# Moving the last output's matmuls and copies behind a data-dependent branch, with the last three stores

## The chip, the cores and the metric

One NeuronCore of a Trainium2 chip runs the kernel; the other cores are idle. The metric is the device time of one execution in microseconds. Five engines run their own instruction streams: TensorE (PE in the profile, with its weight loads as a row of their own, PEld), VectorE (DVE), ScalarE (ACT), GpSimd (POOL) and SyncE (SP), which issues the DMA transfers. They wait for each other through semaphores.

## The reference

A gated linear attention feeds a gated MLP with a spatial product. What is computed:

```python
f = 1.0 / (1.0 + np.exp(-f_logit))
for t in range(S):
    state = f[:, :, t, :, None] * state + np.einsum('bhd,bhe->bhde', k[:, :, t], v[:, :, t])
    y[:, :, t] = np.einsum('bhd,bhde->bhe', q[:, :, t], state)
...
h = np.maximum(x @ w_in, 0.0)
u, v = (h[..., :d_ff // 2], h[..., d_ff // 2:])
v_n = (v - mu) / np.sqrt(var + 1e-06)
v_s = np.einsum('ts,bsd->btd', w_spatial, v_n) + b_spatial[None, :, None]
gated = u * v_s
return (gated @ w_out).astype(np.float32)
```

There are 4 batches, 8 heads of 48 channels, 768 tokens, a model width of 384 and a hidden width of 1024, all in float32.

## The kernel before

The attention runs chunk by chunk with closed-form products in place of the step-by-step recurrence. The MLP works on halves of 384 tokens (`th`) and, for the output, on tiles of 128 tokens (`tt`, three in each half). Every product of the MLP is made in three passes over operands that were split into a high and a low part (`gh`, `gl` for the gated values, `w_outh`, `w_outl` for the weights), and all passes of one output add up in one PSUM bank out of four, `mm0` to `mm3`.

The order of all work is written out by hand in the list `PLAN`: words such as `S:3,1,3` name a step and its indices, and the program runs them one after the other. Each engine executes its own instructions in this order. The steps at the end of the list are:

- `sg`, `sm`, `sh`, `sl` (L607 to L622): for one of four slices of the gated values, bias, product, high part (ACT, `gh`) and low part (DVE, `gl`).
- `Oa:b,th,tt` and `O:b,th,tt` (`part_O`, L631 to L646): the output product of one tile, `gated @ w_out`. `Oa` makes the passes over the first three slices, 9 products; `O` adds the fourth slice, 3 products, or makes all 12 if no `Oa` came before. The very last output, named by `LAST`, is made in two halves of 192 columns in two banks, so it has twice as many products of half the width.
- `oc` (L648 to L653): ACT copies a finished bank to one of three buffers `osb`; the last output is copied half by half.
- `od` (L655 to L658): SP issues the store of an `osb` buffer, 192 KB.
- `end` is no step. It marks the place in `PLAN` where the branch stands.

The closed form of the attention is not exact for extreme forget gates. A check counts such entries, every engine loads the count into a register (`load`, in the middle of the program), and after the steps ahead of `end` there is a branch on it (L716): the first arm repeats everything in a general, slow way; the second arm, the usual one, runs the steps behind `end`. The branch is an instruction of each of the five streams. The first arm lies between the branch and the second arm in every stream. Before the change the second arm holds three stores:

```python
    with tc.If(n_bad > 0) as found:
        ...
    osbs = outputs
    with found.Else():
        for what in PLAN[stop + 1:]:
            run(what)
```

Of the kernel before, what the change touches and what calls it, by code (L numbers as in the profile page):

```python
# [29 lines left out]
P = 128  # L30
# [73 lines left out]
    sg:3,0,0 oc:2,1,0 od:2,1,0 sm:3,0,0 S:3,0,1 sl:3,0,2 sg:3,0,1 S:3,1,3 od:2,0,0 sh:3,0,0 sl:3,0,0 sm:3,0,1  # L104
    U:3,1,0 S:3,1,0 sg:3,1,0 sh:3,0,1 sl:3,0,1 O:3,0,1 oc:3,0,1 od:3,0,1 ur:3,1,0 sm:3,1,0 sh:3,1,0 sl:3,1,0 U:3,1,1
    O:3,0,0 oc:3,0,0 U:3,1,2 ur:3,1,2 ur:3,1,1 sm:3,1,1 O:3,0,2 sh:3,1,1 sl:3,1,1 sm:3,1,2 sh:3,1,2 sl:3,1,2
    oc:3,0,2 U:3,1,3 sg:3,1,3 ur:3,1,3 sm:3,1,3 Oa:3,1,1 Oa:3,1,2 sh:3,1,3 sl:3,1,3 O:3,1,2 oc:3,1,2 Oa:3,1,0
    od:3,0,0 od:3,0,2 O:3,1,0 oc:3,1,0 O:3,1,1 oc:3,1,1 end od:3,1,2 od:3,1,0 od:3,1,1
""".split()


# [36 lines left out]
def tile_kernel(ctx, tc, fkq, fn, vv, w_cv, w_spT, b_sp, out):  # L148
# [6 lines left out]
    ps = ctx.enter_context(tc.tile_pool(name="ps", bufs=1, space=PSUM))  # L155

    def tiles(pool, name, count, shape, dtype=F32):
        return [pool.tile(shape, dtype, name=f"{name}{i}") for i in range(count)]
# [24 lines left out]
    sB = tiles(attn, "sB", 2, [DP, J * D])  # L183
    ysb = attn.tile([P, HD], F32, name="ysb")

    mm = Slots(tiles(ps, "mm", 4, [P, 512]))
    bp = Slots(tiles(ps, "bp", 2, [P, 2, 512]))
    xTs = Slots([tuple(const.tile([P, KX, TH], F32R, name=f"xT{k}{i}") for k in "hl") for i in range(3)])
    vrs = Slots(tiles(const, "vr", 3, [P, G]))
# [5 lines left out]
    gs = gts = osbs = None  # L195
# [459 lines left out]
    def step_od(b, th, tt, row=None):  # L655
        at = (b if row is None else row) * S + th * TH + tt * P
        nc.sync.dma_start(out[bass.ds(at, P)], osbs.of((b, th, tt)))
        osbs.done((b, th, tt))  # L658
# [52 lines left out]


    attn_pool.close()
    outputs = osbs
    dram = ctx.enter_context(tc.tile_pool(name="dram", bufs=1, space=bass.MemoryType.DRAM))
    with tc.If(n_bad > 0) as found:  # L716
        xd = dram.tile([B, HD, S], F32, name="xd")
# [46 lines left out]
        with tc.tile_pool(name="again", bufs=1) as again:  # L764
            open_moe(again)
            xf = again.tile([P, KX, TH], F32, name="xf")
            with tc.For_i(0, B) as b:
# [19 lines left out]
                for th in range(2):  # L787
# [3 lines left out]
                    for tt in range(HU):  # L791
                        step_O("b", th, tt)
                        step_oc("b", th, tt)
                        step_od("b", th, tt, b)
    osbs = outputs
    with found.Else():
        for what in PLAN[stop + 1:]:
            run(what)
# [45 lines left out]
```

## Time and profile before

| what | us |
|---|---|
| median of 3 runs | 352.29 |
| lowest and highest run | 351.34, 353.19 |
| the profiled execution, its own time | 352.25 |
| span of the profiled execution | 350.4 |
| PE busy | 334.1 |
| last copy of the last output ends | 345.1 |
| last store issued | 345.2 |

The span runs from the first to the last instruction in the trace; the execution's own time is 1.85 us longer. Times within the span count from its start. A weight load and its matmul are two instructions, shown under PEld and PE. The instruction streams themselves arrive by DMA, on queues that the profile calls "instruction": q8 with packets of 16 KB, q14 with packets of 8 KB. Rows with a q behind the engine (PEldq, ACTq, SPq) belong to an engine's sequencer, the part that reads the stream and hands work to the engine.

### The profile page before, as it was taken

What the parts mean: (1) busy time and instruction counts of PE and PEld (TensorE: products, weight loads), DVE (VectorE), ACT (ScalarE), POOL (GpSimd) and SP (SyncE); (2) the same over time, 40 slices, a digit from 0 to 9 for tenths busy, and PEclk for the clock granted to TensorE, in tenths of its full rate; (3) what the DMA queues carried; (4) which work ended last, traced back from release to release, by engine and by line L of the source; (5) the groups of instructions that cost most, each with busy time, mean ns of one, the idle gap of its engine ahead of it and who ended that gap; (6) DMA issues with size and microseconds to landing.
All of it is one profiled execution on the core that took longest, in us unless ns stands there. A gap on an engine that the chain in (4) does not pass through costs nothing.

```text
span 350.4 us, 10471 instructions
## 1 busy us (share of the span) xinstructions
PE 334.1 (95%) x4590; PEld 311.7 (89%) x4590; DVE 218.7 (62%) x436; ACT 171.4 (49%) x349; POOL 46.4 (13%) x69
## 2 busy tenths in 40 slices
PE   4689999999999999999999999999999999999993
PEld 3577888989999899999889989999989989999993
DVE  2799879999896966446574675535557657132140
ACT  7776799683645645124544754233443534121231
POOL 3123111303200101003020030012001200001100
PEclk9899999999999999999999999999999999999998
DMA  7849485745323503021630332400101000001012
GB/s 246 331 116 296 153 291 167 281 145 160 91 93 116 204 1 137 2 74 64 178 118 2 125 106 87 159 2 1 47 4 45 4 22 24 22 7 40 23 49 74
DMA packets 14981, 36.01 MB, mean 103 GB/s; under 512 B 1488, under 2 KB 10192, under 8 KB 14928
## 3 DMA queue, kind: packets, MB, share of 16 engines
q1 hardware_dynamic: 14928, 35.26, 30.3%
q8 instruction: 38, 0.62, 0.8%
q14 instruction: 15, 0.12, 0.1%
HBM read 30.54 MB, written 4.72 MB: 101 GB/s over the span
## 4 chain that ended last, share of the span: by engine, by line
PE 89%; DMA 4%; ACT 2%; DVE 1%; issue 1%; SPq 1%; POOL 0%; ACTq 0%; DVEq 0%
PE mm L598 29%; PE mm L636 15%; PE mm L499 14%; PE mm L584 13%; PE bp L385 5%; PE bp L437 4%; PE bp L449 3%; PE bp L409 2%; PE mm L462 2%; DMA fkq<-fkq 2%; DMA words<-w_cv 2%; PE mm L340 2%; POOL fkq L325 0%; DVE fkq L357 0%; SPq L311 0%
## 5 line engine op out<-in xcount | busy, mean ns | idle before, releaser
L607 DVE TENSOR_TENSOR gt<-mm,b_bc 128x384 f32<-128x384 f32 x32 | 17.7, 553 | 37.7 <-PE mm L598 37.7
L598 PE MATMUL mm<-w_sph,vnh 128*128 128x384 f32 x192 | 40.1, 344 | 0.5 <-ACT vr L513 0.5
L598 PE MATMUL mm<-w_spl,vnh 128*128 128x384 f32 x192 | 39.0, 338 | 0.0
L598 PE MATMUL mm<-w_sph,vnl 128*128 128x384 f32 x192 | 39.0, 338 | 0.0
L598 PEld LDWEIGHTS mm<-w_sph,vnh 128*128 128x128 f32 x192 | 33.4, 188 | 0.9 <-ACT vr L513 0.6
L598 PEld LDWEIGHTS mm<-w_spl,vnh 128*128 128x128 f32 x192 | 34.2, 188 | 0.0
L598 PEld LDWEIGHTS mm<-w_sph,vnl 128*128 128x128 f32 x192 | 34.2, 188 | 0.0
L614 POOL TENSOR_TENSOR uT<-gt,uT 128x384 f32<-128x384 f32 x12 | 14.1, 1176 | 149.0 <-DVE gt L607 97.7
L589 ACT ACTIVATE uT<-mm 128x384 f32<-128x384 f32 x32 | 15.5, 489 | 27.4 <-PE mm L584 27.4
L618 ACT CAST gh<-uT 128x384 fp32r<-128x384 f32 x32 | 16.0, 511 | 21.1 <-DVE uT L614 13.4
L622 DVE TENSOR_TENSOR gl<-uT,gh 128x384 fp32r<-128x384 f32 x32 | 17.4, 555 | 13.0 <-ACT gh L618 13.0
L385 PE MATMUL bp<-q,fkq 48*64 48x112 f32 x768 | 23.4, 260 | 0.4 <-DVE fkq L357 0.4
L325 POOL TENSOR_SCALAR fkq<-fkq 112x512 f32<-112x512 f32 (+1 forms) x11 | 16.7, 1515 | 53.4 <-DMA fkq<-fkq 21.7
L584 PE MATMUL mm<-xTh,w_inh 128*128 128x384 f32 x96 | 23.0, 347 | 0.0
L652 ACT COPY osb<-mm 128x384 f32<-128x384 f32 (+1 forms) x25 | 11.4, 465 | 23.6 <-PE mm L636 23.6
L361 DVE TENSOR_TENSOR q<-fkq,F 112x512 f32<-112x512 f32 x24 | 16.4, 684 | 9.6 <-ACT F L346 7.9
L636 PE MATMUL mm<-w_outh,gh 128*128 128x384 f32 (+1 forms) x100 | 22.3, 337 | 0.0
L636 PE MATMUL mm<-w_outh,gl 128*128 128x384 f32 (+1 forms) x100 | 22.1, 333 | 0.0
L584 PE MATMUL mm<-xTh,w_inl 128*128 128x384 f32 x96 | 22.1, 338 | 0.0
L584 PE MATMUL mm<-xTl,w_inh 128*128 128x384 f32 x96 | 22.0, 338 | 0.0
L499 PE MATMUL mm<-w_inh,xTh 128*128 128x512 f32 x72 | 21.8, 410 | 0.0
L636 PE MATMUL mm<-w_outl,gh 128*128 128x384 f32 (+1 forms) x100 | 21.6, 331 | 0.0
(106 smaller groups left out, 704.0 us busy)
## 6 DMA issues: line engine op xcount, KB each, us to landing
fkq<-fkq SPq DMA_DIRECT2D x16, 768.0 KB, 4.6
val<-vv SPq DMA_DIRECT2D x24, 192.0 KB, 4.4
out<-osb SPq DMA_DIRECT2D x24, 192.0 KB, 2.0
fkq<-fkq SPq DMA_DIRECT2D x8, 512.0 KB, 6.0
words<-w_cv SPq DMA_DIRECT2D x4, 768.0 KB, 6.6
fkq<-fn SPq DMA_DIRECT2D x8, 192.0 KB, 3.2
late<-w_cv SPq DMA_DIRECT2D x2, 768.0 KB, 5.7
spat<-w_spT SPq DMA_DIRECT2D x3, 384.0 KB, 5.0
```

Source lines behind the costliest of these rows:

```text
L325: (nc.gpsimd if beside("c", n) else nc.vector).tensor_scalar(f, f, -LOGIT_MOST, None, op0=ALU.max)
L361: nc.vector.tensor_tensor(qs[n % 2][:, :, :, 0:C], *(x.rearrange("p (j c t) -> p j c t", c=T // C, t=C) for x in (parts(n)[2], Fs[n % 2])) ...
L385: nc.tensor.matmul(sc[to, e, cs], k[dr, at:at + C], qs[n % 2][dr, j, chunk], start=True, stop=True)
L499: nc.tensor.matmul(acc, xs[:, c, ut * P:(ut + 1) * P], ws[:, c, G:FF], start=i == 0, stop=i == 3 * KX - 1)
L584: nc.tensor.matmul(acc[:, 0:TH], ws[:, kx, cs], xs[:, kx, :], start=i == 0, stop=i == 3 * KX - 1)
L589: nc.scalar.activation(uTs.take((b, th, c)), mm.of(("u", b, th, c))[:, 0:TH], AF.Relu)
L598: nc.tensor.matmul(acc[:, 0:TH], vns.of((b, ks))[va][:, cs], w_sp_s[wb][:, ks, th * TH:(th + 1) * TH], start=i == 0, stop=i == 3 * KS - 1,)
L607: nc.vector.tensor_tensor(gts.take((b, th, c)), mm.of(("s", b, th, c))[:, 0:TH], b_bc[:, th * TH:(th + 1) * TH], op=ALU.add)
L614: (nc.vector if beside("sm", b, th, c) else nc.gpsimd).tensor_tensor(uT, gts.of((b, th, c)), uT, op=ALU.mult)
L618: nc.scalar.copy(gs.take((b, th, c), HU)[0], uTs.of((b, th, c)))
L622: nc.vector.tensor_tensor(lo, uTs.of((b, th, c)), hi.bitcast(F32), op=ALU.subtract)
L636: nc.tensor.matmul(acc[:, ms], gs.of((b, th, c))[ga][:, ts], w_out_s[wb][:, c, ms], start=c == cs[0] == 0 and ga == wb == 0, stop=c == cs[ ...
```

## The change

The list `PLAN` ends differently, and the four banks and the pools that the second arm uses are kept aside while the first arm is recorded.

```diff
-    oc:3,0,2 U:3,1,3 sg:3,1,3 ur:3,1,3 sm:3,1,3 Oa:3,1,1 Oa:3,1,2 sh:3,1,3 sl:3,1,3 O:3,1,2 oc:3,1,2 Oa:3,1,0
-    od:3,0,0 od:3,0,2 O:3,1,0 oc:3,1,0 O:3,1,1 oc:3,1,1 end od:3,1,2 od:3,1,0 od:3,1,1
+    oc:3,0,2 U:3,1,3 sg:3,1,3 ur:3,1,3 sm:3,1,3 Oa:3,1,2 Oa:3,1,0 sh:3,1,3 sl:3,1,3 O:3,1,2 oc:3,1,2 od:3,0,0
+    od:3,0,2 O:3,1,0 oc:3,1,0 end O:3,1,1 oc:3,1,1 od:3,1,2 od:3,1,0 od:3,1,1
...
-    mm = Slots(tiles(ps, "mm", 4, [P, 512]))
+    banks = tiles(ps, "mm", 4, [P, 512])
+    mm = Slots(banks)
...
-    outputs = osbs
+    mine = mm, gs, gts, osbs
+    mm = Slots(banks)
...
-    osbs = outputs
+    mm, gs, gts, osbs = mine
```

On PE before, ahead of the branch, the last products stand in this order (`mm2` is tile 3,1,0; `mm1` and `mm3` are the halves of the last output, tile 3,1,1, whose other 18 products stand at the head of the final 48):

```order
L636 MATMUL mm2_132<-w_outh_75,gh3_1340 128x384
L636 MATMUL mm2_132<-w_outl_76,gh3_1340 128x384
L636 MATMUL mm2_132<-w_outh_75,gl3_1341 128x384
L636 MATMUL mm1_131<-w_outh_75,gh3_1340 128x192
L636 MATMUL mm1_131<-w_outl_76,gh3_1340 128x192
L636 MATMUL mm1_131<-w_outh_75,gl3_1341 128x192
L636 MATMUL mm3_133<-w_outh_75,gh3_1340 128x192
L636 MATMUL mm3_133<-w_outl_76,gh3_1340 128x192
L636 MATMUL mm3_133<-w_outh_75,gl3_1341 128x192
L716 COMPARE_AND_BRANCH
L724 COMPARE_AND_BRANCH
```

On PE after the change, at the same place (`mm1` is now tile 3,1,2 and `mm3` tile 3,1,0, each begun by 9 products ahead of these rows):

```order
L637 MATMUL mm1_131<-w_outh_75,gh3_1340 128x384
L637 MATMUL mm1_131<-w_outl_76,gh3_1340 128x384
L637 MATMUL mm1_131<-w_outh_75,gl3_1341 128x384
L637 MATMUL mm3_133<-w_outh_75,gh3_1340 128x384
L637 MATMUL mm3_133<-w_outl_76,gh3_1340 128x384
L637 MATMUL mm3_133<-w_outh_75,gl3_1341 128x384
L718 COMPARE_AND_BRANCH
L726 COMPARE_AND_BRANCH
```

And on PE after the change, at the end of the second arm, which was empty of products before (`mm0` and `mm2` are the halves of the last output; 24 products in all, of which the last five stand here):

```order
L637 MATMUL mm2_132<-w_outl_76,gh3_1340 128x192
L637 MATMUL mm2_132<-w_outh_75,gl0_1335 128x192
L637 MATMUL mm2_132<-w_outh_75,gl2_1339 128x192
L637 MATMUL mm2_132<-w_outh_75,gl1_1337 128x192
L637 MATMUL mm2_132<-w_outh_75,gl3_1341 128x192
L718 UNCONDITIONAL_BRANCH
```

Between the product of slice 2 of the gated values and the branch PE had 48 products, 24 of 384 columns and 24 of 192. Now the 24 wide ones stand ahead of the branch and the 24 narrow ones behind it.

On ACT before, around the branch, from the last high part on:

```order
L618 CAST gh3_1340<-uT3_165 128x384
L652 COPY osb2_1349<-mm0_130 128x384
L652 COPY osb1_1348<-mm2_132 128x384
L652 COPY osb0_1347<-mm1_131 128x192
L652 COPY osb0_1347<-mm3_133 128x192
L716 COMPARE_AND_BRANCH
```

And on ACT after the change, at the same place:

```order
L619 CAST gh3_1340<-uT3_165 128x384
L653 COPY osb2_1349<-mm1_131 128x384
L653 COPY osb1_1348<-mm3_133 128x384
L718 COMPARE_AND_BRANCH
L726 COMPARE_AND_BRANCH
```

The two narrow copies now stand in the second arm. SP's stream is the same in both kernels: the three last stores stand in the second arm, in the order 3,1,2, then 3,1,0, then 3,1,1. DVE and POOL have no work moved.

## Rows read from the trace of the kernel before

**Rows 1.** The page's head and part 1: busy us, share of span, instructions.

```profile
span 350.4 us, 10471 instructions
...
PE 334.1 (95%) x4590; PEld 311.7 (89%) x4590; DVE 218.7 (62%) x436; ACT 171.4 (49%) x349; POOL 46.4 (13%) x69
```

**Rows 2.** The chain that ended last, from 340 us: start us, us, what.

```profile
339.92 4.20 PE mm L636 x24
...
344.56 0.55 ACT osb L652 x2
```

**Rows 3.** SP's timeline, stretch 345.2 to 346: start us, us, instruction.

```profile
345.20 0.33 SPq L657 DMA_DIRECT2D out<-osb  x1
```

**Rows 4.** SP's waits: us in total, times, longest us.

```profile
SPq L840 <- DMA out<-osb: 3.2, 2, 2.5
```

**Rows 5.** Stores issued at 338.2, 342.6 and 345.2 us: KB, us to landing.

```profile
out<-osb SPq DMA_DIRECT2D x1, 192.0 KB, 2.0
...
out<-osb SPq DMA_DIRECT2D x1, 192.0 KB, 2.9
...
out<-osb SPq DMA_DIRECT2D x1, 192.0 KB, 4.2
```

**Rows 6.** Queue q8, all; begun 336.0:336.2, 342.85:342.95, 346.34:346.40: packets, MB, share of 16 engines.

```profile
q8 instruction: 38, 0.62, 0.8%
...
q8 instruction: 1, 0.02, 32.5%
...
q8 instruction: 1, 0.02, 82.1%
...
q8 instruction: 1, 0.02, 176.1%
```

**Rows 7.** Packets of q14 begun 346.25:346.33, of the stores' queue begun 347.3:350.

```profile
q14 instruction: 1, 0.01, 24.1%
...
q1 hardware_dynamic: 9, 0.01, 2.2%
```

**Rows 8.** The branch line L716: duration ns min/median/max, first and last start us.

```profile
L716 DVEq COMPARE_BRANCH  x1: 72/72/72, 340.2 to 340.2; - x1
L716 PEldq COMPARE_BRANCH  x1: 3698/3698/3698, 341.9 to 341.9; - x1
L716 DVEq EVENT_SEMAPHORE  x1: 21/21/21, 343.2 to 343.2; - x1
L716 ACTq COMPARE_BRANCH  x1: 50/50/50, 344.8 to 344.8; - x1
L716 ACTq EVENT_SEMAPHORE  x1: 17/17/17, 345.2 to 345.2; - x1
L716 PEldq EVENT_SEMAPHORE  x1: 51/51/51, 345.6 to 345.6; - x1
```

**Rows 9.** Stretch from PE's branch on: us, PE, PEld, DVE, ACT, POOL busy, clock, DMA.

```profile
341.89:344.60 2.71, 2.71 (x19) 2.69 (x17) 0.00 (x0) 0.89 (x3) 0.00 (x0) 1.00 0.25 82
```

**Rows 10.** Weight loads in order of time, from the first of the last 48.

```profile
337.39 0.68 PEld L636 LDWEIGHTS mm<-w_outh,gh 128*128 128x128 f32 x3
...
342.21 0.53 PEld L636 LDWEIGHTS mm<-w_outl,gh 128*128 128x128 f32 x3
342.73 0.53 PEld L636 LDWEIGHTS mm<-w_outh,gl 128*128 128x128 f32 x3
...
344.28 0.19 PEld L636 LDWEIGHTS mm<-w_outl,gh 128*128 128x128 f32 x1
344.39 0.19 PEld L636 LDWEIGHTS mm<-w_outh,gl 128*128 128x128 f32 x1
```

**Rows 11.** The last high and low part of the gated values, ACT and DVE.

```profile
339.59 0.52 ACT L618 CAST gh<-uT 128x384 fp32r<-128x384 f32 x1 [0.99 <-DVE uT L614]
...
340.14 0.56 DVE L622 TENSOR_TENSOR gl<-uT,gh 128x384 fp32r<-128x384 f32 x1 [0.58 <-ACT gh L618]
```

## The prediction

> **What bounds the kernel now.** I read the page first: PE is busy 334.1 of 350.4 us [rows 1], so what the end costs is what stands behind PE's last product. The chain of waits says the same and then stops too early to help: PE's products, then ACT's last two copies, which end at 345.11 [rows 2]. SP issues the last store at 345.20 [rows 3], and the span lasts until 350.4. More than 5 us therefore belong to one store and the closing barrier, and the views of SP and of the DMA queues have to tell why. SP's longest wait at the kernel's end line is 2.5 us, for a store to land [rows 4]. The stores' own rows are the key: the one of 338.2 us landed in 2.0 us, the one of 342.6 in 2.9, the last one in 4.2 [rows 5]. All move the same 192 KB.
>
> What is different about the two slow ones stands in the instruction queue. q8 moved 38 packets in 0.62 MB, 16 KB each [rows 6]; with two instructions for each of PE's 4,590 products [rows 1] that is one packet for about 240 of them, so q8 feeds PE. Its share multiplied by 16 engines and the stretch gives the time of a packet: 32.5% of 16 times 0.2 us is 1.04 us at 336 us, with nothing else moving; 1.31 us for the one begun at about 342.9, and 1.69 us for the one at about 346.37 [rows 6]. I take such a packet to hold one of the 16 DMA engines that long, and a store to be spread over all of them. Behind the last fetch, after 347.3 us, only 9 packets of the store remain [rows 7], and SP waits for exactly these. So **the last store is late because PE's second fetch after the branch fell into it**: 4.2 us against 2.0.
>
> The branch rows tell why PE fetches there. PE's sequencer reached the branch at 341.89 and was held for 3.70 us, until 345.58 [rows 8]. The first fetch begins 1.0 us after the branch; the branch ends 1.37 us after that fetch has ended (341.89 + 1.0 + 1.3 + 1.37 = 345.58). The second fetch begins 0.78 us after the branch ends. DVE shows the same shape, 340.2 to 343.2, 3.0 us [rows 8]. ACT goes on after 0.4 us, so its target was at hand.
>
> One more reading matters. When PE's sequencer reached the branch, 16 products were still to load: the stretch from 341.89 has 17 loads, one of them already under way [rows 9]. The sequencer runs ahead of the engine by 16 products, and waits of queued products do not seem to hold it.
>
> **The change, part by part.** *PE ahead of the branch.* Of the 48 last products 24 wide ones remain. They start at 337.39 as before [rows 10]. Three wide loads take 0.52 us, 0.173 each (342.21 to 342.73) [rows 10]. The first three waited for a high part: their loads took 0.68 us, where narrow ones are 0.11 apart (344.28 to 344.39) [rows 10]; wide products cover about half of that wait, and I leave 0.15 us. The last slice's parts are ready at 340.11 and 340.70 [rows 11]; the products that need them come 19th and 21st, at 340.65 and 341.00, so they wait for nothing. The 25th load could start at 337.39 + 0.15 + 24 x 0.173 = 341.69.
>
> *The branch on PE.* It is reached when 16 products are left, at the 8th load: 337.39 + 0.15 + 7 x 0.173 = 338.75, 3.1 us sooner than before. Its fetch then meets little other traffic: 1.0 + 1.04 + 1.37 = 3.4 us. It ends at 342.18, and the first narrow load follows 0.06 us later, as the arm's first instruction did (345.58 to 345.6 and a little) [rows 8]. So PE stands still for 342.24 - 341.69 = 0.55 us. Bounds for the hold: DVE's 3.0 us and PE's own 3.70 [rows 8], which give a gap of 0.15 to 0.85. I take 3.4, nearest to PE's row, less the contention that the 1.31 us packet showed.
>
> *PE behind the branch.* 24 narrow products at 0.11 us: the last load at 342.24 + 23 x 0.1115 = 344.80, against 344.39 [rows 10]: **+0.4 us**.
>
> *ACT.* Two narrow copies stand in the arm; ACT's branch costs 0.4 us [rows 8] long before they are needed. Nothing is added behind the last product: copies end 345.5, the last store goes out at 345.6.
>
> *SP.* Its stream is unchanged. The stores of 3,1,2 and 3,1,0 go out earlier, since their products no longer stand among the last output's. DVE and POOL lose and gain nothing.
>
> *The last store.* PE's second fetch now starts at 342.18 + 0.78, about 343.0, and is over by 344.3, more than a microsecond before the store's packets. ACT's small fetch (24.1% of 16 times 0.08 us, 0.31 us, begun at about 346.3, 1.0 us after ACT went on) [rows 7] moves forward with ACT's branch as well. The store then lands like the undisturbed one, in 2.0 us or a little less; I take 1.9: 347.5, against 345.2 + 4.2 = 349.4: **-1.9 us net**, that is -2.3 for the landing and +0.4 for PE's gap.
>
> *Sum.* The profiled execution took 352.25 us, 0.04 below the median of the runs. 352.25 - 1.9 = 350.35, say **350.4 us**, 0.5% below the median.
>
> [...] The rows show PE's sequencer 16 products ahead when it takes the branch [rows 9]. [...]
>
> **The rivals.** *1. The stall is not covered (slower).* If the sequencer takes the branch only when the last wide product loads, at 341.5, PE goes on at 341.5 + 3.4 = 344.9 and the last load comes at 345.0 + 2.56 = 347.5, 3.1 us later than now. The last store goes out at 348.3 and lands at 350.2, 0.8 later than now: 353.1 us. It decides from a hold of about 2.3 us that PE does not cover; below that the gain in the landing is larger. Against it: the 16 products of [rows 9]. For it: this is one branch, and the queue may be less full where three products waited. Chance 0.10.
>
> *2. The arm crosses into another 16 KB block.* The 24 products are 48 instructions of about 240 in a packet, so about 1 in 5 places would do it; the spacing of the fetches puts the arm's start well before its block's end. Then a second hold follows, 0.78 + 1.04 + 1.37 = 3.2 us: the last store at 348.8, landing at 350.7, 353.5 us. Chance 0.06.
>
> *3. Another fetch still falls into the last store.* If ACT's small fetch stays near the end, or the three stores now queue on the engine that PE's fetch held, the landing is between 2.0 and 2.9 us [rows 5], not 1.9. With 2.7: 351.2 us. Chance 0.14.
>
> **How the numbers follow.** The forecast has 0.70. Its own range is 349.9 to 350.9: the hold's bounds give -0.4 and +0.3, the landing +-0.1. A median of this kernel can be told from no change at about 0.5%, 1.76 us, so faster means below 350.53. About two thirds of the forecast's chance lie there: 0.50 with a little for a covered stall. Rival 3 and most of rivals 1 and 2 end within 0.5%: same 0.46. Slower by over 0.5% (above 354.05) needs rival 1 or 2 with its dearer bound: 0.04. The range, 349.6 to 351.8, holds the forecast with the spread of the runs and rival 3, and leaves out rivals 1 and 2.
>
> **What would show it.** PE's branch starts near 338.8 and lasts about 3.4 us; q8's last two packets begin near 339.8 and 343; PE idles about half a microsecond between wide and narrow products; the last store is issued near 345.6 and lands in under 2.1 us, so that SP's wait at the end line falls below 1 us. The prediction is wrong if the branch starts after 341, if q8 has a packet after 345, or if the last landing stays above 2.9 us.

## The result, and the profile after

The changed kernel takes 355.03 us (median of 11 runs, 353.2 to 359.09) against 352.11 for the kernel before (11 runs, 350.79 to 353.19): a ratio of 1.0083, with a 95% interval from 1.0056 to 1.011. It is **slower by 0.8%**, where 350.4 us was forecast. The profiled execution took 354.48 us with a span of 352.4. Medians and extremes here and below hold all runs; ratios leave out those over 1.5% longer than the fastest of their kernel, such as the one of 359.09 us here and one of 1130.97 us among the runs of the next version.

The page of the kernel after, head and part 1, against [rows 1]:

```profile
span 352.4 us, 10470 instructions
...
PE 336.4 (95%) x4590; PEld 313.9 (89%) x4590; DVE 219.2 (62%) x436; ACT 171.4 (49%) x349; POOL 46.7 (13%) x69
```

The same 4,590 products keep PE busy 2.3 us longer in this execution. The chain that ended last (start us, us, what) shows what happened at the end, against [rows 2]:

```profile
335.96 1.23 PE mm L585 x7
337.19 4.25 PE mm L637 x24
341.44 2.21 issue
343.65 5.45 PE mm L637 x24
349.10 0.02 issue
349.12 0.32 ACT osb L653
```

Between the 24 wide and the 24 narrow products PE waits 2.21 us for nothing but its own sequencer ("issue"), and the narrow products then take 5.45 us, twice what 24 times 0.11 us would be. The row of PE's branch (duration ns, first and last start us), against [rows 8]:

```profile
L718 PEldq COMPARE_BRANCH  x1: 3367/3367/3367, 340.2 to 340.2; - x1
```

DVE's timeline, the last low part of the gated values, against [rows 11]:

```profile
339.61 0.56 DVE L623 TENSOR_TENSOR gl<-uT,gh 128x384 fp32r<-128x384 f32 x1 [0.58 <-ACT gh L619]
```

And PE's weight loads in order of time, against [rows 10]:

```profile
336.86 0.69 PEld L637 LDWEIGHTS mm<-w_outh,gh 128*128 128x128 f32 x3
...
340.24 0.19 PEld L637 LDWEIGHTS mm<-w_outl,gh 128*128 128x128 f32 x1
340.41 0.19 PEld L637 LDWEIGHTS mm<-w_outh,gl 128*128 128x128 f32 x1
340.59 0.19 PEld L637 LDWEIGHTS mm<-w_outh,gh 128*128 128x128 f32 x1
340.76 0.19 PEld L637 LDWEIGHTS mm<-w_outl,gh 128*128 128x128 f32 x1
340.93 0.19 PEld L637 LDWEIGHTS mm<-w_outh,gl 128*128 128x128 f32 x1
343.65 0.93 PEld L637 LDWEIGHTS mm<-w_outh,gh 128*128 128x128 f32 x4 [2.53 <-issue]
```

The branch was taken at 340.23, with 5 products still to load and not 16, and 0.06 us after the last low part was ready (339.61 + 0.56 = 340.17). Most of its hold of 3.37 us then lies bare: the 25th load comes at 343.65, 2.54 us later than the usual spacing of 0.17 us after the 24th would put it. "Idle" means this lateness from here on, as in the forecast's 0.55 us. The stretches of the wide products, of the hold and of the narrow products (columns as in [rows 9]):

```profile
336.86:341.11 4.25, 4.25 (x26) 4.11 (x25) 2.14 (x4) 1.84 (x5) 0.00 (x0) 1.00 0.14 50
341.11:343.64 2.53, 0.33 (x2) 0.01 (x1) 0.00 (x0) 0.85 (x2) 0.00 (x0) 0.97 0.46 161
343.64:348.70 5.06, 5.05 (x24) 5.05 (x24) 0.00 (x0) 0.32 (x1) 0.00 (x0) 0.50 0.03 8
```

The granted clock is 1.00, falls near the end of the idle stretch (a mean of 0.97 over it), and is 0.50 for all narrow products, half speed. Of the last store, its landing, against [rows 5], and SP's wait for it, against [rows 4]:

```profile
out<-osb SPq DMA_DIRECT2D x1, 192.0 KB, 1.9
```

```profile
SPq L842 <- DMA out<-osb: 0.9, 1, 0.9
```

The store lands in 1.9 us as forecast, but it is issued at 349.5.

### The profile page after: what moved, and what is told of

The parts are those of the page before. It is cut to its first block, busy times and chain, and to the rows that moved or that the text cites. A ratio compares the mean times of both kernels' runs of the same rounds, so it can differ in the third digit from the quotient of the medians.

```text
span 352.4 us, 10470 instructions
## 1 busy us (share of the span) xinstructions
PE 336.4 (95%) x4590; PEld 313.9 (89%) x4590; DVE 219.2 (62%) x436; ACT 171.4 (49%) x349; POOL 46.7 (13%) x69
## 4 chain that ended last, share of the span: by engine, by line
PE 87%; DMA 6%; ACT 2%; DVE 1%; issue 1%; SPq 1%; POOL 0%; DVEq 0%
PE mm L599 29%; PE mm L637 15%; PE mm L500 13%; PE mm L585 13%; PE bp L386 5%; DMA fkq<-fkq 4%; PE bp L438 4%; PE bp L450 3%; PE bp L410 2%; PE mm L463 2%; DMA words<-w_cv 2%; PE mm L341 2%; POOL fkq L326 0%; DVE fkq L358 0%; SPq L312 0%
```

## The experiments

Executions begin the last 48 products at different times, 336.3 to 341.3 us in the profiles below, because the work ahead of them varies by a few microseconds, and the runs' times vary too. So I measured the end by itself: the stretch from the load of the first of the last 48 products to the end of the span. It is 13.05 us before and 15.53 after, a difference of 2.5 us; the medians differ by 2.9.

### The order without the branch

```diff
-    od:3,0,2 O:3,1,0 oc:3,1,0 end O:3,1,1 oc:3,1,1 od:3,1,2 od:3,1,0 od:3,1,1
+    od:3,0,2 O:3,1,0 oc:3,1,0 O:3,1,1 oc:3,1,1 end od:3,1,2 od:3,1,0 od:3,1,1
```

> The new order of the products with all of them still ahead of the branch. Theory (PE's branch takes a 3.4 us fetch and a second fetch 0.8 us after it; the first is harmless where no product waits behind it, the second delayed the last store of the kernel before): PE's branch starts near 342.6, about 0.7 us later than before, its second fetch near 347, after the last store's packets, so that the store lands in 2.0 to 2.4 us instead of 4.2; PE has no hold ahead of its last product. 350.0 to 350.6 us. Rival (the order itself, wide products first, costs time, and the branch is not to blame for the slower kernel): near 354.

Measured: the stretch is 10.97 us, the last store lands in 2.2 us, and PE's second fetch begins 2.69 us after that store's issue. In the runs a ratio of 1.0006 (0.9964 to 1.0049) and a median of 352.63 us, so the 350.0 to 350.6 us of the expectation were missed, but the interval ends below that of the changed kernel. A second time, with more runs:

> The new order with all products ahead of the branch, once more, with more runs. Theory: as in its first profile 11.0 us from the first of the last 48 products to the end, 2.1 us less than the kernel before, so about 350.1 us or a ratio of 0.994. Rival (the second profile shows the second fetch in the last store, because the branch moves from run to run): 13 us and a ratio of 1.000.

The stretch is 11.09 us as expected, the landing 2.3 us; the ratio is 0.9984 (0.9951 to 1.0017) where 0.994 was expected, the median 350.47 us against 352.21. PE's branch in the two profiles:

```profile
L718 PEldq COMPARE_BRANCH  x1: 4338/4338/4338, 343.5 to 343.5; - x1
```

```profile
L718 PEldq COMPARE_BRANCH  x1: 4418/4418/4418, 341.4 to 341.4; - x1
```

The hold is even longer than in the changed kernel, 4.3 and 4.4 us, and costs nothing, for no product stands behind it. So the order is not what costs; what stands behind the branch is. The first fetch fell into another store here, the second-last one (KB, us to landing, first of the two profiles; 4.2 us in the second too):

```profile
out<-osb SPq DMA_DIRECT2D x1, 192.0 KB, 4.2
```

### The branch earlier

In two more versions a part of every output's products stands ahead of the branch and the rest behind it. In the first, 18 wide products stand ahead:

```diff
-    ... sh:3,1,3 sl:3,1,3 O:3,1,2 oc:3,1,2 od:3,0,0 od:3,0,2 O:3,1,0 oc:3,1,0 end O:3,1,1 ...
+    ... sh:3,1,3 sl:3,1,3 od:3,0,0 od:3,0,2 end O:3,1,2 oc:3,1,2 O:3,1,0 oc:3,1,0 O:3,1,1 ...
```

> The branch is moved ahead of the products with the last slice: 18 wide products ahead, 6 wide and 24 narrow behind. Theory (PE's sequencer itself waits for a product's operands, so in the changed kernel it reached the branch only when the last low part was ready, 0.06 us after it; else it runs up to 16 products ahead): the branch starts about 1.0 us after the first of the 18 products, ends 3.4 us later, PE is idle about 1 us, the clock stays full, 350.9 us. Rival (the sequencer runs only about 5 products ahead of wide ones): the branch starts 2.4 us after the first product, PE is idle 2.3 us, the clock falls, 352.4 us or more.

In the second, the narrow ones are begun ahead of the branch as well:

```diff
-    ... Oa:3,1,2 Oa:3,1,0 sh:3,1,3 sl:3,1,3 O:3,1,2 oc:3,1,2 od:3,0,0 od:3,0,2 O:3,1,0 oc:3,1,0 end O:3,1,1 ...
+    ... Oa:3,1,1 Oa:3,1,2 Oa:3,1,0 sh:3,1,3 sl:3,1,3 od:3,0,0 od:3,0,2 end O:3,1,2 oc:3,1,2 O:3,1,0 oc:3,1,0 O:3,1,1 ...
```

> All three outputs are begun ahead of the branch (18 narrow, then 18 wide products, none with the last slice), the 12 products with the last slice stand behind it. Theory: the sequencer reaches the branch with 16 wide products queued, about 2.5 us after the first product; the hold of 3.4 us leaves PE idle 0.5 us; the clock stays full; the last store goes out 0.5 us later than before the change and lands in 2 us: 350.5 us. Rival (5 products ahead): PE idle over 2 us, 352.4 us or more.

Measured, first kernel: the branch starts 1.14 us after the first product with 11 products queued, again 0.10 us after a low part (the second-last, ready at 340.16; branch at 340.26); idle 1.8 us where 1 was expected; the clock stays at 1.00; stretch 12.31 us; ratio 1.0028 (0.9985 to 1.0072), median 352.78 us and not 350.9. Second kernel: the branch starts 2.39 us after the first product with 16 queued; idle 0.94 us where 0.5 was expected; stretch 11.79 us; ratio 0.9997 (0.9956 to 1.0037), median 351.89 us and not 350.5. Both holds were longer than the 3.4 us that the expectations took, 3.75 and 3.78 us, and so both idle times. The places of the branch are those of the theory, 1.0 and 2.5 us forecast; neither count of queued products is the rival's 5. The second kernel's last store, and the two that were issued ahead of it within one microsecond (KB, us to landing):

```profile
out<-osb SPq DMA_DIRECT2D x1, 192.0 KB, 1.9
```

```profile
out<-osb SPq DMA_DIRECT2D x2, 192.0 KB, 1.9
```

Three stores issued within 1.03 us land in 1.9 us each. PE's second fetch is over 0.3 us after the first of them is issued, before the two others.

### The wait, taken away

```diff
-                        acc[:, ms], gs.of((b, th, c))[ga][:, ts], w_out_s[wb][:, c, ms],
+                        acc[:, ms], gs.of((b, th, 2 if (b, th, c, ga) == (3, 1, 3, 1) else c))[ga][:, ts], w_out_s[wb][:, c, ms],
```

> The changed kernel in which the products of the last half with the low part of the last slice read the low part of another slice instead (the low part of the last slice is made and left out of the output). Theory (PE's sequencer waits for a product's operands before it queues the product, and the branch comes behind the last such wait): the last wait is now for the last high part, so the branch starts 0.06 us after that CAST ends, about 2.8 us after the first of the last 48 products instead of 3.4, with about 9 products queued instead of 5, and PE is idle about 2.0 us instead of 2.6. Rival (the queue takes only 5 wide products, whatever they wait for): 3.4 us, 5 products and 2.6 us as in the changed kernel.

ACT's timeline, the last high part, and PE's branch:

```profile
340.83 0.51 ACT L619 CAST gh<-uT 128x384 fp32r<-128x384 f32 x1 [0.99 <-DVE uT L615]
```

```profile
L718 PEldq COMPARE_BRANCH  x1: 3761/3761/3761, 341.4 to 341.4; - x1
```

The high part is ready at 341.34 and the branch starts at 341.40, 2.78 us after the first product instead of 3.37, with 8 products queued. PE is idle 2.36 us and not the expected 2.0, since the hold is 3.76 us and not 3.4; the third profile of the changed kernel, with a hold of 3.77 us, has 2.87. The branch moved by 0.59 us and the idle time by 0.51: the wait for operands set the branch's place, to a tenth of a microsecond.

### The hold filled with work

```diff
-    od:3,0,2 O:3,1,0 oc:3,1,0 end O:3,1,1 oc:3,1,1 od:3,1,2 od:3,1,0 od:3,1,1
+    od:3,0,2 O:3,1,0 oc:3,1,0 W0 D:12 W1 end O:3,1,1 oc:3,1,1 od:3,1,2 od:3,1,0 od:3,1,1
...
-            nc.tensor.matmul(mm.of("warm")[:, 0:2 * P], junk[:, 0:P], junk[:, 0:2 * P], start=True, stop=True)
+            nc.tensor.matmul(mm.of("warm"), junk[:, 0:P], junk, start=True, stop=True)
```

> The changed kernel with 12 products of 512 columns on a constant tile, whose result nobody reads, queued between the last wide product and the branch, so that PE works through the hold (12 times 0.213 us). Theory (the hold costs 2.3 us, and as much again because the clock falls to half after the idle stretch and the 24 narrow products then take 0.213 instead of 0.11 us each): the clock stays full, the narrow products take 0.11 us, the last store goes out some 2.2 us sooner: 352.3 us. Rival (the narrow products are slow for another reason, the fetched instructions or the queue running dry): 0.21 us each again, 354.5 us.

Stretches from the first filler product to the arm, and of the 24 narrow products (columns as in [rows 9]):

```profile
341.70:344.69 2.99, 2.86 (x13) 1.10 (x12) 0.00 (x0) 0.83 (x2) 0.00 (x0) 1.00 0.40 138
344.69:347.46 2.77, 2.76 (x24) 2.75 (x24) 0.00 (x0) 0.32 (x1) 0.00 (x0) 1.00 0.04 14
```

Eleven of the fillers take 2.54 us in the chain that ended last, where 11 times 0.213 would be 2.34. With PE at work through the hold the clock is 1.00 and the 24 products take 2.77 us instead of 5.06. The kernel does more and its stretch is 13.56 us, 2.0 less than in the changed kernel's first profile; in the runs 1.0027 (0.9995 to 1.0059), median 353.09 us where 352.3 was expected. The same products on fetched instructions take 2.77 us at a clock of 1.00 and 5.06 at 0.50, so they were slow by the clock. That the filler kept the clock up is not shown by one profile: below, it stays at 1.00 in two of three profiles without a filler.

### The second fetch and the last store

```diff
-    od:3,0,0 od:3,0,2 O:3,1,0 oc:3,1,0 O:3,1,1 oc:3,1,1 end od:3,1,2 od:3,1,0 od:3,1,1
+    od:3,0,0 od:3,0,2 O:3,1,0 oc:3,1,0 O:3,1,1 oc:3,1,1 W0 D:8 W1 end od:3,1,2 od:3,1,0 od:3,1,1
```

> The kernel before with 8 more products of 256 columns on a constant tile, whose result nobody reads, at PE's end, just ahead of the branch. Theory (PE's second fetch delays the last store of the kernel before): the branch starts 1 to 2 us later, near 343.5 where the last 48 products begin at 337.4, so its second fetch starts after the last store's packets; the store lands in 2.0 to 2.7 us instead of 4.2, and the stretch from the first of the last 48 products to the span's end is 11.3 to 11.9 us instead of 13.1, though PE has more to do. Rival (three stores within 2.6 us hinder each other, and the fetch is not to blame): the landing stays at 4.2 us and the stretch at 13.1.

The last store of this kernel:

```profile
out<-osb SPq DMA_DIRECT2D x1, 192.0 KB, 2.5
```

The landing is 2.5 us and the stretch 11.33 us, though PE has eight more products: 1.7 us less than the kernel before showed in its first profile. In the runs 1.0018 (0.9972 to 1.0063), no gain. More profiles of the kernel before show what its first one is worth:

> The kernel before once more, for a second profile. Theory: PE's branch again with 16 products queued, its second fetch again within the last store, a landing of about 4 us, and 13 us from the first of the last 48 products to the span's end. Rival (that landing was an accident of one execution): 2 us and 11 us.

> The kernel before, a third profile. Theory (whether PE's second fetch falls into the last store depends on some tenths of a microsecond: it began 1.17 us after the store's issue in the first profile and 1.66 us in the second): a landing of 2.0 to 2.5 us where the fetch begins over 1.5 us after the store's issue, and about 4 us where it begins sooner; the stretch from the first of the last 48 products to the end is 11.3 or 13.1 us accordingly. Rival (the first landing had another cause): no such tie.

> The kernel before, a fourth profile, as the third: 11.3 us from the first of the last 48 products to the end where PE's second fetch begins over 1.5 us after the last store's issue, 13.1 us where it begins sooner.

The last store's landing in the second, third and fourth profile, in this order:

```profile
out<-osb SPq DMA_DIRECT2D x1, 192.0 KB, 2.4
```

```profile
out<-osb SPq DMA_DIRECT2D x1, 192.0 KB, 4.2
```

```profile
out<-osb SPq DMA_DIRECT2D x1, 192.0 KB, 3.5
```

| kernel before | hold of PE's branch, us | 2nd fetch after last store's issue, us | landing, us | stretch, us |
|---|---|---|---|---|
| first profile | 3.70 | 1.17 | 4.18 | 13.05 |
| second | 3.88 | 1.66 | 2.44 | 11.31 |
| third | 3.59 | 1.20 | 4.19 | 13.07 |
| fourth | 3.35 | 1.18 | 3.46 | 12.36 |

The tie holds: where the fetch begins 1.2 us after the store's issue the store suffers, at 1.7 us hardly. How long the fetch lasts matters too: 1.69 us in the first profile, 1.66 in the third, 0.95 in the fourth, and in all three the store lands 1.32 to 1.33 us after the fetch has ended. What is left of the stretch without the landing is 8.87 to 8.90 us in all four. The second profile's expectation of a landing of about 4 us failed, and the fourth's of 13.1 us was 0.7 too long. The long landing is not a property of the kernel but of three of the four executions profiled, decided by half a microsecond.

The 0.3 to 0.6 us between a landing of 1.9 and one of 2.2 to 2.5 go with another fetch. In all 14 profiles of this document the last store lands in 1.9 us where neither instruction queue begins a fetch between its issue and its landing (seven profiles); in the four with 2.2 to 2.5 us a packet of q14 begins 0.7 to 1.1 us after the issue, and PE's fetch 1.7 us after it or later. A small fetch near the end is one of the two causes that the forecast's third rival named; it was not tested by itself.

### The changed kernel again

> The changed kernel once more, for a second profile and more runs. Theory: PE's branch 0.06 us after the last low part, hold 3.4 us, idle 2.3 us or a little more; where the clock falls in the hold the narrow products take 0.213 us each, and the stretch from the first of the last 48 products to the end is 15.5 us; if the fall came later, at most 2.4 us less. Against the kernel before +2.0 to +2.9 us. Rival (the clock's fall was an accident): 13.1 us and no difference to the kernel before.

> The changed kernel, a third profile. Theory: PE idle 2.6 us behind the 24 wide products; a landing of 1.9 us; 13.2 us from the first of the last 48 products to the end where the clock stays full, 15.5 us where it falls in the idle stretch, 13.2 to 15.5 where it falls among the narrow products. Rival (the hold moves from run to run): another idle time.

Hold and narrow products of the second profile (columns as in [rows 9]):

```profile
341.60:344.28 2.68, 0.33 (x2) 0.02 (x1) 0.00 (x0) 0.85 (x2) 0.00 (x0) 1.00 0.44 155
344.28:347.05 2.77, 2.76 (x24) 2.75 (x24) 0.00 (x0) 0.32 (x1) 0.00 (x0) 1.00 0.05 13
```

| kernel after | branch after first product, us | hold, us | PE idle, us | clock of the narrow products | landing, us | stretch, us |
|---|---|---|---|---|---|---|
| first profile | 3.37 | 3.37 | 2.54 | 0.50 | 1.85 | 15.53 |
| second | 3.37 | 3.54 | 2.69 | 1.00 | 1.86 | 13.20 |
| third | 3.37 | 3.77 | 2.87 | 1.00 | 1.86 | 13.42 |

The branch stands at the same place to 0.01 us and PE is idle 2.5 to 2.9 us each time; the clock fell in one of three. The second set of runs gives 1.006 (1.002 to 1.010), +2.1 us, as the theory said; its profile has the full clock and 13.2 us, as the rival said. How often the clock falls is not settled by three profiles.

## Why the prediction was wrong

**The step that failed is the start in "The branch on PE", "reached when 16 products are left, at the 8th load", built on the reading that "waits of queued products do not seem to hold it".** The 16 were read rightly from [rows 9], but the second half was wrong. In the kernel before the last waits lay far behind when the branch came up: the low part was ready at 340.70 [rows 11] and the branch at 341.89, so no wait was open, and the row could not tell the two apart. In the changed kernel the last product that waits, for the low part, is the 21st, and the branch stands behind the 24th. In these profiles the sequencer did not go past a product whose operand was missing: branch 0.06 us behind the low part in the changed kernel, 0.06 us behind the high part once the low part was not awaited, 0.10 us behind an earlier low part when the branch stood earlier, and 16 or 17 products ahead only where the last wait was over, by 0.15 us or more. The term was 1.36 us after the first product; it measured 3.37.

**The hold in "The branch on PE" was right**: 3.4 forecast, 3.37 to 3.77 measured. (By its own terms it ends at 342.16 and not 342.18, a slip of 0.02.) What it left bare was not: 0.55 us of idle time forecast, 2.54 to 2.87 measured. The forecast's own bound for this gap, 0.15 to 0.85, varied the hold and took the start for certain. The first rival had this mechanism, with a chance of 0.10 and 353.1 us, and named its reason, a queue less full where products wait; that reason deserved more. Of the forecast's three signs of being wrong none shows at face value, since they were set in times of the span: the branch started at 340.2, q8's last packet began at 344.89, the landing was 1.9 us. Counted from the first of the 48 products, 0.53 us earlier here, the second sign is there: the packet begins 8.03 us after it, where 345 stood for 7.61.

**"PE behind the branch" was mis-sized in one of three profiles**: 0.11 us for each narrow product holds at the full clock (24 in 2.77 us at 1.00), 0.21 at half (24 in 5.06 at 0.50). Nothing in the forecast priced the clock, though an idle stretch had been considered. The trace of before has such a stretch, near its start: PE has no product from 10.23 to 12.63 us, and the clock then is at half until 16.0 (columns as in [rows 9]):

```profile
10.23:12.58 2.35, 0.00 (x0) 0.00 (x0) 1.92 (x3) 2.32 (x5) 0.62 (x2) 1.00 0.98 367
12.63:16.00 3.37, 3.37 (x80) 3.04 (x84) 2.66 (x5) 2.93 (x6) 0.00 (x0) 0.50 0.93 345
```

PE had only just begun to work there, at 4.95 us, so the rows do not settle what the clock would do at the end; but they give a reason for a rival in which the narrow products take twice as long, 2.3 us more. The stretches of narrow products have a clock of 1.00 or 0.50, and the changed kernel's profiles differ there: one fall in three.

**"The last store" was right for the execution it was read from and wrong as a gain.** The landing fell from 4.2 to 1.9 us, as forecast. The cause, PE's second fetch, is shown by the four profiles of before, where the landing follows the fetch's end; the kernel with eight more products agrees, and so do the two landings of 4.2 us of the second-last store in the new order, with the first fetch in them. But the 2.3 us stood for every execution; over four profiles the landing before averages (4.18 + 2.44 + 4.19 + 3.46) / 4 = 3.57 us, so the gain is about 1.7, as far as four executions tell.

The sum of the first pair of profiles: the store goes out 12.61 instead of 7.80 us after the first product, 4.8 later (2.54 idle; 23 times 0.100 = 2.30 by the clock; 0.15 more from the last product's load to the store; less 0.18 of a wait that wide products cover); the landing gives back 2.3; together +2.5 us. Over all profiles the stretch is 14.05 us after (three) and 12.45 before (four), +1.6 us; the runs say +2.9 and, by 1.006, +2.1. At a full clock the stretches alone give +0.9 us (13.31 less 12.45), with the fall +3.1 (15.53 less 12.45); the runs lie between, as they would if the clock fell in over half of the executions. That it does is not shown.

"ACT", the copies' branch being hidden, was right: it was taken at 341.54 and the first narrow copy came at 346.7. The two earlier stores went out sooner, 0.6 and 2.1 us counted from the first of the 48 products, and gained nothing: the end waits for the last one.

The version closest to beating both is the new order with all products ahead of the branch: 10.97 and 11.09 us of stretch against 11.31 to 13.07 before, because PE's second fetch begins 2.7 us after the last store's issue in both profiles. Its ratios lie below those of the changed kernel; against the kernel before both intervals hold 1, so the gain that the stretches promise, 1.4 us or 0.4%, is not shown by the runs.

## What to carry to other kernels

PE's branch was held for 3.4 to 4.4 us in these profiles, with a code fetch in the hold: in the first profile before and the first after, the fetch began 1.0 us after the branch started, and the hold ended 1.37 us after the fetch had ended. Work behind it waited that long, less what the engine still had queued (3.37 less 5 products of 0.17 us leaves 2.5 in the first profile after); and nothing was queued behind a product whose operand was not ready yet (the branch came 0.06 to 0.10 us after the operand). Put the last wait well ahead of the branch, or leave everything that somebody waits for ahead of it. And where a gain hangs on two transfers that miss or meet each other by half a microsecond, take several profiles before counting it.

## What was not expected of the hardware

PE's sequencer stopped at the first product whose operand was not ready, and a branch behind it waited too (it started 0.06 us after the operand was ready, in four profiles). The hold of the same branch varied from 3.35 to 4.42 us; it was longest, 4.34 and 4.42, where the fetch came while the second-last store was under way. One code fetch of 16 KB, while a 192 KB store ran, kept that store from landing for 2.3 us beyond its usual 1.9. After 2.21 us without a product PE's clock stood at half, 0.50, in one profile of the changed kernel; after 2.36 and 2.53 us in the two others it was full, 1.00. Near the kernel's start, where PE has only just begun to work (first product at 4.95 us), it fell to half during 2.1 to 2.8 us without a product, or within 0.7 us after, in all eleven profiles that have such a stretch there: at 12.58 us, 2.35 us into it, in the first profile before, and at 12.37 us, 2.14 us into it, in the first after.
